# Moving one tile's PE transpose ahead of a pair of score steps in the start of an attention and MLP kernel

## The chip, the cores and the metric

The kernel runs on one core of a Trainium2 chip. The metric is device time in microseconds. All timed runs with more than one execution were fast, at a granted TensorE clock of 1.00.

## The reference, cut to what matters

```python
xn = _layernorm(x)                                   # x: 2048 x 512
q  = (xn @ wq) -> 32 heads of 2048 x 128
p  = softmax(q @ k_cache.T * 128 ** -0.5)            # 2048 keys per head
s  = concat_heads(p @ v_cache) @ wo
g  = silu(relu(xn @ w1 + b1) ** 2 @ w2 + b2)
return x + s * g
```

## The kernel before

Each engine has a program in a fixed order, and waits on semaphore counts where it needs another engine's result. The long steady state takes 512 query rows at a time through each head: scores on TensorE into `psA`, an exponential on ScalarE from `psA` into `pT`, then `pT` against `v` ("PV") on TensorE into `psO`. `psA` has two halves, so scores `pi` have to wait for exponential `pi - 2`.

Only the first head is different. Its 512 query rows come in four tiles of 128, counted from 0 here, and work starts on a tile as soon as it is there. A tile is normalised and scaled on VectorE (`xn_t`), transposed on TensorE, copied to `xnT` by VectorE, and projected for the first and the second head. Tile `qt` then makes two steps, scores `2*qt` and `2*qt + 1`, one per half of the keys.

```python
def first_transpose(i):                              # four 128x128 PE transposes
    for c in range(NDC):
        t_xT[i] = E(PE, partial(_peT, out=bankF(1)..., in_=xn_t[:, i, ...], ident=ident[:]),
                    deps=[t_xn[i], t_ident, tok_xT[0][i - 1] if i else None], ...)

# gen_scores(pi), first head only
qt, b = divmod(pi, 2)
for c in range(NKT // 2):                            # eight matmuls of 128 columns
    t = E(PE, partial(_mm_shared, out=psA[...], lhsT=kT[...], rhs=qt_sb[:, 0, qt*P:(qt+1)*P], ...),
          deps=[t_k0[b], t_q0[qt], t_exp[pi - 2] if pi >= 2 else None], ...)
...
t_exp[pi] = E(AC, partial(_act, out=pT[:, pi % NPT, :], in_=psA[...], func=ACT.Exp, ...),
              deps=[t, t_PV[pi - NPT] if pi >= NPT else None])

# the emission order of the start (cut)
second_proj(1)
gen_pv(0)
ln_bn(0, 3, 0, HD)
gen_scores(2)
ln_scale(0, 2)
first_transpose(2)
ln_bn(0, 3, HD, D)
gen_scores(3)
first_copy(2)
ln_rstd(0, 3, n=2)
first_proj(2)
first_evac(2)
second_proj(2)
gen_pv(1)
ln_scale(0, 3)
gen_scores(4)
first_transpose(3)
first_copy(3)
gen_scores(5)
```

The softmax here doesn't subtract the row's maximum and nothing guards it: scores larger than these inputs give would overflow.

Of the kernel before, what the change touches and what calls it, by code (L numbers as in the profile page):

```python
# [214 lines left out]
def bass_recurrent_scan__mha_block_cached__dense_activation_squared_relu__prompt_kernel(  # L215
# [87 lines left out]
    def bankF(i):  # L303
        return psF[:, i * 512:(i + 1) * 512]
# [45 lines left out]
    def ln_bn(j, i, c0=0, c1=D):  # L350
        jt = j * TPB + i
        k = 6 if c0 else 0
        t_bn[jt] = E(DV, partial(_bn_stats, out=st_t[:, i, k:k + 6], in_=x_ln[:, i, c0:c1]),
                     deps=[t_xl[jt], t_xn.get(jt - TPB), t_xr.get(jt - TPB)])
# [15 lines left out]
    def ln_scale(j, i):  # L370
        jt = j * TPB + i
        t_xn[jt] = E(DV, partial(_ts, out=xn_t[:, i, :], in0=x_ln[:, i, :],
                                 scalar1=mv_t[:, i, 0:1], scalar2=rstd[:, i:i + 1],
                                 op0=ALU.subtract, op1=ALU.mult),
                     deps=[t_xr[jt], t_xnr.get(jt - TPB)])
# [49 lines left out]
    def first_transpose(i):  # L425
        for c in range(NDC):
            t_xT[i] = E(PE, partial(_peT, out=bankF(1)[:, 0:256].bitcast(BF16)[:, c * P:(c + 1) * P],
                                    in_=xn_t[:, i, c * P:(c + 1) * P], ident=ident[:]),
                        deps=[t_xn[i], t_ident, tok_xT[0][i - 1] if i else None],
                        inc=(c == NDC - 1))  # L430
        t_xnr[i] = t_xT[i]
# [93 lines left out]
    def gen_scores(pi):  # L525
        g, k = divmod(pi, NPR)
        s2, i = pi % 2, g % NSL
        assert t_kfill[g] is not None and t_evac[g] is not None
        t = None
        if g == 0:  # L530
            qt, b = divmod(pi, 2)
            for c in range(NKT // 2):
                t = E(PE, partial(_mm_shared, out=psA[:, s2 * 1024 + c * P:s2 * 1024 + (c + 1) * P],
                                  lhsT=kT[:, 0, (b * NKT // 2 + c) * P:(b * NKT // 2 + c + 1) * P],
                                  rhs=qt_sb[:, 0, qt * P:(qt + 1) * P], start=True, stop=True),
                      deps=[t_k0[b], t_q0[qt], t_exp[pi - 2] if pi >= 2 else None],
                      inc=(c == NKT // 2 - 1))
        else:
            for n in range(2):
                tt = 2 * k + n  # L540
                t = E(PE, partial(_mm, out=psA[:, s2 * 1024 + n * 512:s2 * 1024 + (n + 1) * 512],
                                  lhsT=kT[:, i, tt * P:(tt + 1) * P], rhs=qt_sb[:, g % NQS, :],
                                  start=True, stop=True),
                      deps=[t_exp[pi - 2] if pi >= 2 else None, t_kfill[g], t_evac[g],
                            t_bankF[0] if pi == 0 else None],
                      inc=(n == 1))
        if k == NPR - 1:
            t_S_last[g] = t
        t_exp[pi] = E(AC, partial(_act, out=pT[:, pi % NPT, :],
                                  in_=psA[:, s2 * 1024:(s2 + 1) * 1024],  # L550
                                  func=ACT.Exp, scale=SM_SCALE),
                      deps=[t, t_PV[pi - NPT] if pi >= NPT else None])
# [373 lines left out]
    second_proj(1)  # L926
    gen_pv(0)
    ln_bn(0, 3, 0, HD)
    gen_scores(2)
    ln_scale(0, 2)  # L930
    first_transpose(2)
    ln_bn(0, 3, HD, D)
    gen_scores(3)
    first_copy(2)
# [104 lines left out]
```

## Time and profile before

| | before |
|---|---|
| median of 3 runs | 1238.17 us (1237.9 to 1238.31) |
| span of the profiled run | 1236.1 us |
| TensorE busy | 99% |
| ScalarE busy | 85% |
| PV 0 starts | 9.30 us |
| scores 5 start | 12.83 us |

The times below are read as starts of groups of matmuls. The profile models the end of a matmul, so a short wait between two groups on TensorE can lie under the modelled tail of the first one. It is then seen only where the distance between two starts exceeds the usual slot: 0.45 us for eight matmuls of 128 columns, 0.23 us for four. Below, such a usual distance is called a slot. In profile lines PE is TensorE's matmuls, PEld its weight loads, DVE VectorE, ACT ScalarE and POOL GpSimd; brackets at the end give the idle time just before and what ended it.

### The profile page before, as it was taken

To read this page: it belongs to the slowest core of one execution; us is meant where nothing else is said; L and a number is where in the kernel's file an instruction comes from. 1 tells how busy PE (TensorE), PEld (TensorE's weight loads), DVE (VectorE), ACT (ScalarE), POOL (GpSimd) and SP (SyncE) were. 2 spreads that over 40 slices of the span, in tenths; PEclk is the share of its full clock that TensorE was granted. 3 is DMA by queue.
4 is the path that set the end of the run, shared out by engine and by line. 5 is a ranking of instruction groups with operands and counts; after the bars stand their busy time and mean duration, and the time that the engine had idled before them with its cause. 6 is when DMAs were issued, how large, how long until landed. Compare 5 with 4: busy or idle time off the path is not lost.

```text
span 1236.1 us, 26728 instructions
## 1 busy us (share of the span) xinstructions
PE 1220.8 (99%) x11678; PEld 819.1 (66%) x11885; DVE 472.8 (38%) x953; ACT 1054.6 (85%) x1044; POOL 32.0 (3%) x73
## 2 busy tenths in 40 slices
PE   9999999999999999999999999999999999999998
PEld 7666666666666666666666666666666666666665
DVE  4453323244435332334444532333344333324333
ACT  7888888888888888888888888888888888888885
POOL 1010000000002000000000200000000000000000
PEclk9999999999999999999999999999999999999999
DMA  9999998787879897768779878787778788878771
GB/s 211 203 245 194 187 178 134 130 144 143 140 152 171 144 158 129 141 138 144 133 135 169 171 138 144 141 148 133 134 146 148 146 154 158 137 134 146 145 124 31
DMA packets 686868, 185.41 MB, mean 150 GB/s; under 512 B 673536, under 2 KB 685568, under 8 KB 686752
## 3 DMA queue, kind: packets, MB, share of 16 engines
q1 hardware_dynamic: 684656, 179.62, 80.0%
q0 software_dynamic: 1424, 3.81, 1.2%
q8 instruction: 94, 1.54, 0.6%
q10 hardware_dynamic: 672, 0.26, 0.1%
q14 instruction: 22, 0.18, 0.0%
HBM read 96.60 MB, written 2.10 MB: 80 GB/s over the span
## 4 chain that ended last, share of the span: by engine, by line
PE 98%; issue 1%; DVE 0%; DMA 0%; POOL 0%; DVEq 0%
PE psO L157 38%; PE psA L152 35%; PE psF L152 25%; PE psA L157 0%; DMA x_ln<-in_A_x_dram 0%; DVE out_t L165 0%; PE psF L196 0%; DVE tmp_t L175 0%; PE psO L152 0%; DVE xnT L179 0%; DVE st_t L200 0%; POOL rstd L165 0%; DVE xn_t L171 0%; DVE mv_t L204 0%; DVE ve_t L171 0%
## 5 line engine op out<-in xcount | busy, mean ns | idle before, releaser
L161 ACT ACTIVATE pT<-psA 128x1024 bf16<-128x1024 f32 x1024 | 1044.5, 1024 | 162.9 <-PE psA L152 117.6
L157 PEld LDWEIGHTS psO<-v_sb,pT 128*128 128x128 bf16 x8192 | 547.9, 98 | 240.3 <-issue 12.4
L157 PE MATMUL psO<-v_sb,pT 128*128 128x129 bf16 x8192 | 631.2, 220 | 0.5
L152 PE MATMUL psA<-qt_sb,kT 128*128 128x512 bf16 x1840 | 562.9, 379 | 10.1
L179 DVE COPY o_un<-psO 128x258 f32<-128x258 f32 x256 | 97.4, 422 | 399.5 <-PE psO L157 398.8
L152 PE MATMUL psF<-xnT,wq_sb 128*128 128x512 bf16 (+1 forms) x508 | 165.7, 374 | 0.4 <-DVE xnT L179 0.2
L152 PE MATMUL psF<-wo_all,oT 128*128 128x512 bf16 x478 | 163.2, 379 | 0.1
L152 PEld LDWEIGHTS psA<-qt_sb,kT 128*128 128x128 bf16 x2032 | 157.0, 98 | 0.0
L179 DVE CAST qt_sb<-psF 128x512 bf16<-128x512 f32 (+1 forms) x130 | 88.0, 677 | 97.3 <-PE psF L152 93.7
L165 DVE TENSOR_TENSOR o_bf<-o_un,rden 128x512 bf16<-128x512 f32 x128 | 88.6, 692 | 4.7 <-DVE rden L183 0.3
L152 PEld LDWEIGHTS psF<-xnT,wq_sb 128*128 128x128 bf16 x520 | 50.3, 98 | 60.0 <-issue 0.3
L171 DVE TENSOR_SCALAR r_t<-psF,b1f 128x512 bf16<-128x512 f32 x56 | 42.0, 750 | 117.4 <-PE psF L152 117.4
L152 PEld LDWEIGHTS psF<-wo_all,oT 128*128 128x128 bf16 x480 | 46.9, 98 | 56.4
L152 PE MATMUL psF<-xnT,w_sb 128*128 128x512 bf16 x224 | 77.1, 379 | 0.0
L152 PE MATMUL psF<-w_sb,h2T 128*128 128x512 bf16 x223 | 73.7, 379 | 0.0
L152 PEld LDWEIGHTS psF<-xnT,w_sb 128*128 128x128 bf16 x224 | 21.9, 98 | 26.4
L152 PEld LDWEIGHTS psF<-w_sb,h2T 128*128 128x128 bf16 x224 | 21.9, 98 | 26.4
L165 DVE TENSOR_TENSOR z_t<-psF,b2bc 128x512 f32<-128x512 f32 x16 | 11.1, 692 | 67.2 <-PE psF L152 62.0
L165 DVE TENSOR_TENSOR acc<-psF,acc 128x512 f32<-128x512 f32 x28 | 19.3, 689 | 30.0 <-PE psF L152 30.0
L208 POOL DMA_DIRECT2D out_dram<-out_t x12 | 6.7, 554 | 891.1 <-DVE out_t L165 891.1
L165 DVE TENSOR_TENSOR h2T<-r_t 128x512 bf16<-128x512 bf16 x56 | 23.8, 426 | 1.9
L183 DVE RECIPROCAL rden<-o_un 128x4 f32<-128x4 f32 x128 | 22.9, 179 | 4.4
(47 smaller groups left out, 165.2 us busy)
## 6 DMA issues: line engine op xcount, KB each, us to landing
v_sb<-in_A_v_cache_dram SPq DMA_DIRECT2D x127, 512.0 KB, 4.7
wq_sb<-in_A_wq_dram SPq DMA_DIRECT2D x127, 128.0 KB, 3.1
wo_all<-in_A_wo_dram SPq DMA_DIRECT2D x4, 1024.0 KB, 6.4
w_sb<-in_B_w_dram SPq DMA_DIRECT2D x14, 256.0 KB, 4.1
oT<-o_bf SPq DMA_TRANSPOSE x128, 4.0
x_t<-in_A_x_dram POOLq DMA_DIRECT2D x16, 128.0 KB, 3.5
kT<-in_A_k_cache_dram SPq DMA_TRANSPOSE x127, 4.5
x_ln<-in_A_x_dram SPq DMA_DIRECT2D x15, 128.0 KB, 4.0
```

Of the source, the lines that this page charges most:

```text
L152: return e.matmul(out, lhsT, rhs, start=start, stop=stop)
L157: return e.matmul(out, lhsT, rhs, start=start, stop=stop, skip_group_check=True)
L161: return e.activation(out, in_, func, bias=bias, scale=scale)
L165: return e.tensor_tensor(out, in0, in1, op)
L171: return e.tensor_scalar(out, in0, scalar1=scalar1, scalar2=scalar2, op0=op0, op1=op1)
L179: return e.tensor_copy(out, in_)
L183: return e.reciprocal(out, in_)
L208: return e.dma_start(out, in_)
```

## The change

The transpose of tile 2 (the third tile) goes ahead of scores 2, the first scores of its predecessor, tile 1. The intent: its copy on VectorE then runs while TensorE does scores 2 and 3, and the projection behind them need not wait for it.

```diff
     gen_pv(0)
     ln_bn(0, 3, 0, HD)
-    gen_scores(2)
     ln_scale(0, 2)
     first_transpose(2)
+    gen_scores(2)
     ln_bn(0, 3, HD, D)
     gen_scores(3)
```

## The prediction

> **What bounds the kernel now.** I read the page first: busy shares, then the chain that ended last.
>
> ```profile
> PE 1220.8 (99%) x11678; PEld 819.1 (66%) x11885; DVE 472.8 (38%) x953; ACT 1054.6 (85%) x1044; POOL 32.0 (3%) x73
> ...
> PE 98%; issue 1%; DVE 0%; DMA 0%; POOL 0%; DVEq 0%
> PE psO L157 38%; PE psA L152 35%; PE psF L152 25%; PE psA L157 0%; DMA x_ln<-in_A_x_dram 0%; DVE out_t L165 0%; PE psF L196 0%; DVE tmp_t L175 0%; PE psO L152 0%; DVE xnT L179 0%; DVE st_t L200 0%; POOL rstd L165 0%; DVE xn_t L171 0%; DVE mv_t L204 0%; DVE ve_t L171 0%
> ```
>
> TensorE's matmuls are 98% of the chain; ScalarE is busy 85%. The view of who waited for whom says whether anything but TensorE's own order holds it back:
>
> ```profile
> ACT pT L161 <- PE psA L152: 117.6, 397, 0.5
> ...
> PEld psO L157 <- issue: 12.4, 62, 0.2
> ```
>
> ScalarE waits for TensorE 397 times, while the steady state's weight loads wait only for "issue" (62 pauses of at most 0.2 us, no producer named). No DMA stands among TensorE's releasers. So a delay or gain in the start that survives until about 16 us should reach the end at its own size, neither grown nor absorbed.
>
> The change lies in that start: the first head pair, whose four query tiles are normalised, transposed and scored one by one. Timeline of before for PE, weight loads left out; columns are start, us, engine, line, op, tiles:
>
> ```profile
> 9.30 0.63 PE L157 MATMUL psO<-v_sb,pT 128*128 128x129 bf16 x8
> 9.77 0.61 PE L157 MATMUL psA<-qt_sb,kT 128*128 128x128 bf16 x8
> 10.21 0.39 PE L196 MATMUL psF<-ident,xn_t 128*128 128x128 bf16 x4
> 10.44 0.61 PE L157 MATMUL psA<-qt_sb,kT 128*128 128x128 bf16 x8
> 11.12 0.40 PE L152 MATMUL psF<-xnT,wq_sb 128*128 128x128 bf16 x4
> 11.35 0.39 PE L152 MATMUL psO<-xnT,wq_sb 128*128 128x128 bf16 x4
> 11.58 0.62 PE L157 MATMUL psO<-v_sb,pT 128*128 128x129 bf16 x8
> 12.03 0.61 PE L157 MATMUL psA<-qt_sb,kT 128*128 128x128 bf16 x8
> 12.60 0.40 PE L196 MATMUL psF<-ident,xn_t 128*128 128x128 bf16 x4
> 12.83 0.61 PE L157 MATMUL psA<-qt_sb,kT 128*128 128x128 bf16 x8
> ```
>
> In order: PV 0; scores 2; transpose of tile 2; scores 3; tile 2's two projections; PV 1; scores 4; transpose of tile 3; scores 5. From starts of groups in a row without a wait: eight matmuls take a slot of 0.45 us, four take 0.23. Two slots are longer. Scores 3 to projection is 0.68, so 0.23 of waiting; scores 4 to the next transpose is 0.57, so 0.12 of waiting. These waits end with other engines' work, in VectorE's and ScalarE's timelines:
>
> ```profile
> 9.44 0.40 DVE L171 TENSOR_SCALAR xn_t<-x_ln,mv_t,rstd 128x512 bf16<-128x512 bf16 x1
> 9.75 0.42 DVE L200 BATCH_NORM_STATS2 st_t<-x_ln 128x6 f32<-128x256 bf16 x1
> 10.64 0.42 DVE L179 COPY xnT<-psF 128x512 bf16<-128x512 bf16 x1 [0.47 <-PE psF L196]
> ...
> 12.13 0.41 DVE L171 TENSOR_SCALAR xn_t<-x_ln,mv_t,rstd 128x512 bf16<-128x512 bf16 x1 [0.28 <-POOL rstd L165]
> ```
>
> ```profile
> 10.41 1.94 ACT L161 ACTIVATE pT<-psA 128x1024 bf16<-128x1024 f32 x2 [0.25 <-PE psA L157]
> 12.68 1.94 ACT L161 ACTIVATE pT<-psA 128x1024 bf16<-128x1024 f32 x2 [0.33 <-PE psA L157]
> ```
>
> The copy of tile 2's transpose ends at 11.06 and the projection starts 0.06 later: that is the 0.23. The scaling of tile 3 ends at 12.54, its transpose starts at 12.60: that is the 0.12. ScalarE runs exponentials 2 and 3 from 10.41 to 12.35, each 1.02 long and so 0.92 apart, with idle gaps of 0.25 and 0.33 in front of this pair and the next.
>
> **What the Trainium skill says.** "TensorE: Matmul & The Clock Gate", section "What overlaps and what doesn't", has matmuls in strict order. The trace agrees: the groups run in program order, and TensorE waits at 11.12 although PV 1, behind the projection, needs only an exponential that ended near 10.16. So a transpose put first makes the scores wait with it. The same page, "Part 4: PE-mode transpose", gives about 275 ns for a 128x128 transpose in a kernel and notes that a DVE copy must follow. Here one takes 219 ns, they are pipelined, and four hold a slot of 0.23; I use that. "Perfetto Trace Analysis", "Tensor Engine Instruction (MATMUL, LD_WEIGHTS)", says that a matmul's reported end is estimated and that semaphore propagation is hidden. Therefore I use start-to-start times and measured hand-over gaps: VectorE to TensorE 0.05 to 0.06, TensorE's last end to its reader 0.03 to 0.04, and ScalarE to TensorE about 0.06 (PV 0 starts at 9.30, and the exponential before it ran from 8.22 to 9.24).
>
> **The change part by part.** No instruction is added or removed. The four transposes of tile 2 (a 0.23 slot) exchange places with the eight matmuls of scores 2 (0.45). VectorE's, ScalarE's and POOL's orders stay the same.
>
> 1. A new wait. TensorE's slot after PV 0 opens at 9.77, but tile 2's scaled rows end at 9.84; plus 0.05, the transposes start at 9.89. Wait: 0.12.
> 2. Scores 2 start at 9.89 + 0.23 = 10.12 instead of 9.77, 0.35 later, and end at 10.73. Scores 3 start at 10.57 instead of 10.44.
> 3. The transposes end at 9.89 + 0.40 = 10.29; the copy runs from 10.33 to 10.75 instead of 10.64 to 11.06, 0.31 earlier. VectorE is free then, its statistics ending at 10.17.
> 4. The projection is ready at 10.81, but TensorE comes to it only at 10.57 + 0.45 = 11.02. The old wait of 0.23 vanishes; against the new 0.12, TensorE is 0.10 to 0.11 ahead (11.02 for 11.12).
> 5. Projections and PV 1 follow without a wait; scores 4 start at 11.93 for 12.03. They need exponential 2 finished: it now starts at 10.73 + 0.03 = 10.76 and ends at 11.78, ready at 11.84. It fits with 0.09 to spare.
> 6. Tile 3's chain (aggregate, POOL's two small operations, scaling) hangs on the copy of step 3 and moves by the same 0.31, so its rows end near 12.23 and can be used at 12.28. TensorE reaches its transpose at 12.38: the old 0.12 is gone too, and 0.22 is gained at this point.
> 7. Then scores 5, in TensorE's order due at 12.61. They write the psA half that exponential 3 reads. The exponentials were delayed by 0.35, so it ends at 12.70 instead of 12.35 and releases it at 12.76. A new wait of 0.15 takes most of it back: scores 5 start at 12.76 for 12.83. Net gain **0.07 us**.
> 8. Afterwards exponential 4 starts at 12.60 (0.92 after exponential 3; scores 4 are done at 12.54) for 12.68. Everything up to scores 6 follows TensorE's order with 0.07 less; ScalarE has 0.88 of idle before 15.49, so its delay is used up.
>
> Sum: +0.12 (new wait for the scaling), -0.23 (copy), -0.12 (tile 3's scaling), +0.15 (psA half), about -0.08; from the rounded starts -0.07. On the path that is 1238.17 - 0.07 = **1238.1 us**.
>
> **The rivals.**
> - The wait for the scaling is the only thing that survives. If the delayed exponentials hold TensorE longer (a hand-over of 0.15 instead of 0.06, or the second exponential slower while VectorE copies from PSUM), scores 5 start later than 12.83 and the change costs up to about 0.12. For it: margins in steps 5 and 7 are under 0.1 us. Against it: the hand-over was seen as 0.06. It would make 1238.2 to 1238.3.
> - The full gain of 0.22 survives because scores 5 don't wait. That needs exponential 3 free by 12.61, so ending at 12.55 at most, but two exponentials starting after scores 2 take 1.94, from 10.76. It would make 1237.95; I give it little.
> - ScalarE is the engine that sets the start, so its 0.35 delay comes through whole: 1238.5. Against it stand the 0.25, 0.33 and 0.88 us of ScalarE idle while it waits for TensorE; the second and third absorb it.
> - A shift of a tenth of a microsecond changes how later DMAs meet, or the 62 issue pauses. The waits of before show no DMA on TensorE's path, and the pauses belong to a stream whose length is unchanged. One or two pauses more or fewer would be 0.2 to 0.4 us either way, as much as the repeated runs differ by.
>
> **Range and chances.** The three runs spread over 0.41 us (1237.9 to 1238.31), so a median of a few runs moves by perhaps 0.2. All the mechanisms lie between -0.22 and +0.35. Allowing another 0.3 for a differing build, I take 1237.5 to 1238.8. A 2% change is 24.8 us; the entire stretch from the moved transpose to scores 6 (10.21 to 14.85) is under 5 us, so even losing it twice over would not be 2%. Within 2%: 0.99, the rest split evenly.
>
> **What would show it right or wrong.** In the changed profile: the transposes of tile 2 first at about 9.89, VectorE's scaling as releaser; scores 2 near 10.12; exponential 2 near 10.76 with idle near 0.6 instead of 0.25; the copy at 10.33 and no wait of the projection on xnT, which starts at 11.02; tile 3's transpose near 12.38; scores 5 near 12.76, held by pT's exponential; the steady state's waits unchanged. Wrong in sign if scores 5 start after 12.83. Wrong altogether if the time differs by over 0.7 us: that would need a difference in the steady state, for which I see no cause.

## The result

| | before | changed |
|---|---|---|
| median, same rounds, 6 runs each | 1238.02 us | 1238.09 us |
| lowest to highest | 1237.9 to 1238.31 | 1237.8 to 1238.53 |
| ratio, 95% interval | | 1.0 (0.9988 to 1.0013) |

A ratio is the mean time of one kernel's fast runs over that of the other's fast runs of the same rounds, so it is not quite the ratio of the medians. 1238.09 lies on the predicted 1238.1. That match is luck and confirms nothing: 1238.1 was 0.07 below a median of before that was itself 1238.17 then and 1238.02 here, and in these rounds the changed kernel's median is 0.07 above it. The effect is small against runs of one kernel, which differ by several tenths. The trace has to say whether the reasons hold.

First the page of the changed kernel, its busy shares and its chain that ended last:

```profile
PE 1231.9 (100%) x11885; PEld 819.5 (66%) x11885; DVE 472.3 (38%) x953; ACT 1053.4 (85%) x1044; POOL 32.0 (3%) x73
...
PE 99%; DVE 0%; issue 0%; POOL 0%; DVEq 0%; POOLq 0%
```

TensorE seems to have worked 11.1 us more. It has not. The page of before lists 11678 matmuls beside 11885 weight loads, this one 11885 of both: 207 matmul records were missing from the first trace. The change has no part in it: three later traces of the changed kernel list 11678 again (1220.7 to 1221.0 us busy); in all, exactly 207 are missing in nine of the 13 traces. A difference in busy time is to be read with the counts beside it.

The view of who waited for whom in the changed kernel:

```profile
ACT pT L161 <- PE psA L152: 118.0, 397, 0.5
...
PEld psO L157 <- issue: 12.5, 62, 0.2
```

The steady state is as before: 118.0 for 117.6 us, and again 62 pauses. Now the start, TensorE's timeline without weight loads in the changed kernel:

```profile
9.48 0.63 PE L157 MATMUL psO<-v_sb,pT 128*128 128x129 bf16 x8
10.07 0.40 PE L196 MATMUL psF<-ident,xn_t 128*128 128x128 bf16 x4
10.30 1.06 PE L157 MATMUL psA<-qt_sb,kT 128*128 128x128 bf16 x16
11.20 0.39 PE L152 MATMUL psF<-xnT,wq_sb 128*128 128x128 bf16 x4
11.42 0.39 PE L152 MATMUL psO<-xnT,wq_sb 128*128 128x128 bf16 x4
11.64 0.62 PE L157 MATMUL psO<-v_sb,pT 128*128 128x129 bf16 x8
12.10 0.61 PE L157 MATMUL psA<-qt_sb,kT 128*128 128x128 bf16 x8
12.54 0.39 PE L196 MATMUL psF<-ident,xn_t 128*128 128x128 bf16 x4
12.95 0.62 PE L157 MATMUL psA<-qt_sb,kT 128*128 128x128 bf16 x8
```

VectorE's scaling and copy of tile 2 and scaling of tile 3, then ScalarE's exponentials 2 to 5, then the weight loads of scores 5, same run:

```profile
9.62 0.40 DVE L171 TENSOR_SCALAR xn_t<-x_ln,mv_t,rstd 128x512 bf16<-128x512 bf16 x1
...
10.51 0.42 DVE L179 COPY xnT<-psF 128x512 bf16<-128x512 bf16 x1 [0.16 <-PE psF L196]
...
11.99 0.41 DVE L171 TENSOR_SCALAR xn_t<-x_ln,mv_t,rstd 128x512 bf16<-128x512 bf16 x1
```

```profile
10.95 3.77 ACT L161 ACTIVATE pT<-psA 128x1024 bf16<-128x1024 f32 x4 [0.61 <-PE psA L157]
```

```profile
12.94 0.45 PEld L157 LDWEIGHTS psA<-qt_sb,kT 128*128 128x128 bf16 x8 [0.18 <-ACT pT L161]
```

The whole stretch is 0.18 us later than before, because PV 0 itself, which stands ahead of the moved instructions, started at 9.48 and not at 9.30. Counted from PV 0 the picture is clean. "Predicted" is the time of the prediction less its 9.30:

| us after PV 0 starts | before | predicted | changed |
|---|---|---|---|
| transpose of tile 2 | 0.91 | 0.59 | 0.59 |
| scores 2 | 0.47 | 0.82 | 0.82 |
| copy of tile 2 | 1.34 | 1.03 | 1.03 |
| exponential 2 | 1.11 | 1.46 | 1.47 |
| projection of tile 2 | 1.82 | 1.72 | 1.72 |
| scores 4 | 2.73 | 2.63 | 2.62 |
| transpose of tile 3 | 3.30 | 3.08 | 3.06 |
| scores 5 | 3.53 | 3.46 | 3.47 |
| PV 4 | 6.44 | | 6.39 |
| last 58 matmuls of the kernel | 1217.94 | | 1217.89 |

The last row comes from these lines, of before and of the changed kernel:

```profile
1227.24 5.86 PE L152 MATMUL psA<-wo_all,oT 128*128 128x512 bf16 x58
```

```profile
1227.37 5.86 PE L152 MATMUL psA<-wo_all,oT 128*128 128x512 bf16 x58
```

Scores 5 start 0.06 us earlier, PV 4 (the one behind scores 6 and 7) and the last matmuls 0.05. In absolute time the last matmuls are 0.13 later (1227.37 for 1227.24), which is the 0.18 of PV 0 less the 0.05.

### The profile page after: what moved, and what is told of

Same layout as the page of the kernel before. It is cut to its first block, busy times and chain, and to the rows that moved or that the text cites. A ratio compares the mean times of both kernels' runs of the same rounds, so it can differ in the third digit from the quotient of the medians.

```text
span 1236.2 us, 26935 instructions
## 1 busy us (share of the span) xinstructions
PE 1231.9 (100%) x11885; PEld 819.5 (66%) x11885; DVE 472.3 (38%) x953; ACT 1053.4 (85%) x1044; POOL 32.0 (3%) x73
## 4 chain that ended last, share of the span: by engine, by line
PE 99%; DVE 0%; issue 0%; POOL 0%; DVEq 0%; POOLq 0%
PE psO L157 38%; PE psA L152 36%; PE psF L152 25%; PE psA L157 0%; DVE out_t L165 0%; PE psO L196 0%; DVE tmp_t L175 0%; PE psF L196 0%; PE psO L152 0%; DVE qt_sb L179 0%; POOL warm L187 0%; POOL mhalf L187 0%; DVEq L119 0%; POOLq L1024 0%
## 5 line engine op out<-in xcount | busy, mean ns | idle before, releaser
L161 ACT ACTIVATE pT<-psA 128x1024 bf16<-128x1024 f32 x1024 | 1043.4, 1023 | 163.7 <-PE psA L152 118.0
L152 PE MATMUL psA<-qt_sb,kT 128*128 128x512 bf16 x2032 | 604.4, 379 | 0.0
L152 PE MATMUL psF<-xnT,wq_sb 128*128 128x512 bf16 (+1 forms) x520 | 168.7, 374 | 0.1
L165 DVE TENSOR_TENSOR z_t<-psF,b2bc 128x512 f32<-128x512 f32 x16 | 11.1, 691 | 67.2 <-PE psF L152 67.2
```

The source lines that it names most:

```text
L152: return e.matmul(out, lhsT, rhs, start=start, stop=stop)
L161: return e.activation(out, in_, func, bias=bias, scale=scale)
L165: return e.tensor_tensor(out, in0, in1, op)
```

## The experiments

My theory: the change swaps waits in TensorE's queue with a sum of about -0.06 us, and this reaches the end undiminished, under a variation of the start that has nothing to do with it. The main rival: the order affects PV 0's start too, and the change costs what the medians show.

**The two kernels again.** Both unaltered, more than once; first one of each.

> The changed kernel, unaltered, to get a second profile and a narrower interval. My theory: the change gives TensorE 0.06 us, measured from the start of PV 0 (L157 psO x8, the first one): scores 5 start 3.47 us after it (before: 3.53), the steady state some 0.05 us earlier than before. What the first profile showed on top, PV 0 itself 0.18 us later, is a variation of the first key load and not of the change: here PV 0 may start anywhere from 9.25 to 9.55. Time against before: ratio 1.0 within 0.0005. Rival, that the change really costs 0.07 us as the medians read: PV 0 again 0.18 later, and a ratio above 1.

> The kernel before, unaltered, for a second profile. Theory: scores 5 start 3.53 us after PV 0 again, the projection of tile 2 at 1.82 and the transpose of tile 3 at 3.30 after it, whatever PV 0's own start (9.25 to 9.55). Rival, that the order decides PV 0's start: PV 0 at 9.30 again.

After again: 1237.97 us median of 5 runs, before in the same rounds 1237.97 of 9, ratio 0.9999 (0.9986 to 1.0013). Scores 5 stood at 3.47 after PV 0 (13.02 and 9.55) in the changed kernel and at 3.53 (12.81 and 9.28) in the one before; before again had the projection at 1.82, but the transpose of tile 3 at 3.29 where 3.30 was expected. But PV 0 started at 9.55 and 9.28. With the kernels below, all three with the old order now had PV 0 at 9.28 to 9.30 and all six with the new at 9.42 to 9.62. That spoke for the rival.

> The kernel before, unaltered. In the profiles so far PV 0 started at 9.28 to 9.30 in all three kernels with the old order, at 9.42 to 9.62 in all six with the new. Theory: chance, since everything there runs before the moved instructions: it goes with the moment at which TensorE's matmuls get short (314 to 219 ns) and with the landing of the first keys. Then PV 0 can start past 9.4 here too. Rival, that the order sets it: 9.28 to 9.30 again in this and in before_4.

> The changed kernel, unaltered. Theory: PV 0's start varies with the clock's moment and the key load alone, so it can be near 9.3 here; and whatever it is, scores 5 start 3.47 after it. Rival, that the order sets it: 9.42 or later again in this and in after_4, and the times of these rounds 0.1 to 0.2 us above the kernel before.

> As before_3: a further profile and five times of the kernel before.

> As after_3: a further profile and five times of the changed kernel.

The pattern did not hold. In these four it is the other way round: PV 0 at 9.68 and 9.61 in the kernel before, at 9.25 and 9.26 in the changed one.

| | PV 0 starts | scores 5 after it | last matmuls after it | median of 5 |
|---|---|---|---|---|
| before_3 | 9.68 | 3.52 | 1217.94 | 1238.14 us |
| before_4 | 9.61 | 3.53 | 1217.94 | 1237.99 us |
| after_3 | 9.25 | 3.46 | 1217.89 | 1238.01 us |
| after_4 | 9.26 | 3.46 | 1217.89 | 1237.91 us |

All four are "same" (ratios 0.9999 to 1.0). The rival falls: either order has PV 0 early and late. What makes the start vary shows in TensorE's timeline of the first key transposes. This is before_4, where the transposes were short early (219 ns in the median) and the second half of the keys landed late:

```profile
6.57 0.62 PE L196 MATMUL psO<-ident,kT 128*128 128x128 bf16 x8 [0.47 <-DMA kT<-in_A_k_cache_dram]
```

And this is early_rows, described next, without a wait for a DMA there but with slow matmuls: the same eight transposes took 0.90 instead of 0.62, and the median transpose of the keys 314 ns where a fast one takes 219.

```profile
6.08 0.90 PE L196 MATMUL psO<-ident,kT 128*128 128x128 bf16 x8
```

So both the landing of a load and the moment at which the matmuls become short move PV 0, over 9.25 to 9.68 us in all runs: 0.43 us, seven times the effect of the change. Two pairs of traces separate them. The transposes of tile 0 start at 5.67 both in after_4 and in early_rows (whose own edits act later), here in this order, without a wait for a DMA:

```profile
5.67 0.40 PE L196 MATMUL psF<-ident,xn_t 128*128 128x128 bf16 x4
```

```profile
5.67 0.62 PE L196 MATMUL psF<-ident,xn_t 128*128 128x128 bf16 x4
```

The first projection then starts at 6.68 and 6.89, PV 0 at 9.26 and 9.47: slow matmuls alone, 0.21 us. In before_again and before_4 the same transposes start at 5.69 and 5.70 and take 0.40; then the key transposes start at 5.93 and, with their load late, at 6.57, PV 0 at 9.28 and 9.61: a late load alone, 0.33 us.

**Rows of tile 2 earlier.** The new wait before the transpose is for the scaled rows. They can be had sooner: the small variance operation on VectorE, and the scaling before tile 3's statistics. To the changed kernel:

```diff
-    ln_rstd(0, 2)
+    ln_rstd(0, 2, eng=DV)
...
-    ln_bn(0, 3, 0, HD)
     ln_scale(0, 2)
+    ln_bn(0, 3, 0, HD)
```

> The change, and tile 2's scaled rows made earlier: its small variance operation on VectorE instead of POOL, and its scaling ahead of the first half of tile 3's statistics. Theory: the new wait of 0.12 before the transpose of tile 2 falls to about 0.02, so everything up to exponential 3 is 0.10 earlier, and scores 5 start 3.36 after PV 0 (changed kernel 3.47, before 3.53), still held by exponential 3. Rival, that exponential 3 isn't what holds scores 5: they follow the transpose of tile 3 directly, whose rows aren't earlier, and stay near 3.47. The time is 0.1 lower than the changed kernel's at most, which the rounds can't resolve: ratio 1.0 to before within 0.0005.

TensorE in this run, the transpose of tile 2 and scores 5:

```profile
9.96 0.40 PE L196 MATMUL psF<-ident,xn_t 128*128 128x128 bf16 x4
...
12.84 0.62 PE L157 MATMUL psA<-qt_sb,kT 128*128 128x128 bf16 x8
```

With PV 0 at 9.47, the transpose is at 0.49 (wait 0.02) and scores 5 at 3.37, against 3.47. PV 4 is at 6.29 and the last matmuls at 1217.79, 0.10 earlier than in the changed kernel and 0.15 earlier than before. The rival, that scores 5 depend on tile 3's rows and stay, is out. The time: 1237.79 us median of 5, against 1237.97 of before and of the changed kernel in the same rounds; ratio to before 0.9998 (0.9986 to 1.0011). The result is correct. In the trace it is the best correct version run here; by the interval of its times it is the same.

**Exponential 3 made short, with both orders.** If the wait of scores 5 for exponential 3 takes back most of the gain, shortening that one exponential must help the changed kernel and do nothing for the one before. The result is wrong in 512 columns of one step. The same edit was made to both kernels:

```diff
+    t_pT3 = E(GP, partial(_memset, out=pT[:, 3, 512:1024], val=1.0))
...
-        t_exp[pi] = E(AC, partial(_act, out=pT[:, pi % NPT, :],
-                                  in_=psA[:, s2 * 1024:(s2 + 1) * 1024],
+        w_exp = 512 if pi == 3 else 1024
+        t_exp[pi] = E(AC, partial(_act, out=pT[:, pi % NPT, 0:w_exp],
+                                  in_=psA[:, s2 * 1024:s2 * 1024 + w_exp],
                                   func=ACT.Exp, scale=SM_SCALE),
-                      deps=[t, t_PV[pi - NPT] if pi >= NPT else None])
+                      deps=[t, t_PV[pi - NPT] if pi >= NPT else t_pT3 if pi == 3 else None])
```

> The change, with exponential 3 taken over 512 of its 1024 columns (wrong result on purpose; the rest of its tile is filled with ones by POOL early), so that it ends about 0.45 us sooner and frees its half of psA before scores 5 come to it. Theory: the wait of scores 5 for exponential 3 is what takes back 0.15 to 0.18 us; without it they follow tile 3's transpose directly and start 3.29 us after PV 0 instead of 3.47. Rival, something else holds scores 5 (tile 3's rows, TensorE's order): 3.47 unchanged.

> The kernel before with the same short exponential 3 (wrong result on purpose). Theory: there exponential 3 was done long before scores 5 came, so nothing moves: scores 5 start 3.53 us after PV 0. With the run of the changed kernel the gain of the change is then 0.24 us in place of 0.06. Rival, a shorter exponential helps both alike: scores 5 here near 3.35.

Transpose of tile 3 and scores 5, first in the changed order, PV 0 at 9.62:

```profile
12.68 0.39 PE L196 MATMUL psF<-ident,xn_t 128*128 128x128 bf16 x4
12.90 0.61 PE L157 MATMUL psA<-qt_sb,kT 128*128 128x128 bf16 x8
```

and in the old order, PV 0 at 9.28:

```profile
12.57 0.40 PE L196 MATMUL psF<-ident,xn_t 128*128 128x128 bf16 x4
12.80 0.61 PE L157 MATMUL psA<-qt_sb,kT 128*128 128x128 bf16 x8
```

Changed: scores 5 one slot after the transpose, at 3.28 instead of 3.47. Before: 3.52, nothing moved. With this wait away the change is worth 3.52 - 3.28 = 0.24 us, and it keeps that: PV 4 at 6.19 against 6.43, the last matmuls at 1217.70 against 1217.94. This is the term that turns a gain of 0.24 into one of 0.06. The two single times, 1237.97 (changed order) and 1237.88 us, don't show it; their starts differ by 0.34 us.

**The same move one step further.** The next transpose, of tile 3, also put ahead of its predecessor's scores. To the changed kernel:

```diff
     ln_scale(0, 3)
-    gen_scores(4)
     first_transpose(3)
+    gen_scores(4)
```

> The change, and the same move one step further on: tile 3's transpose ahead of scores 4. Theory: its rows are usable 2.97 us after PV 0, while TensorE comes to it at 2.62, so the new wait is 0.35 us; scores 4 start at 3.20 instead of 2.62, scores 5 at 3.65 instead of 3.47, no longer held by exponential 3 (free at 3.46). A loss of 0.18 against the changed kernel: the same move costs where the rows are not ready, and the copy's wait that it could save isn't there. Rival, that putting a transpose first always helps because the copy runs sooner: scores 5 at 3.47 or less.

The transpose of tile 3, then scores 4 and 5 merged, with PV 0 at 9.42:

```profile
12.40 0.40 PE L196 MATMUL psF<-ident,xn_t 128*128 128x128 bf16 x4 [0.20 <-DVE xn_t L171]
12.63 1.06 PE L157 MATMUL psA<-qt_sb,kT 128*128 128x128 bf16 x16
```

The transpose waits until 2.98 (expected 2.97), and scores 4 start at 3.21. Scores 5 are the second half of a merged group, so one slot of 0.45 later at 3.66 (worked out; expected 3.65). PV 4 is at 6.57, 0.18 later than in the changed kernel, and the last matmuls at 1218.07, 0.18 later too. The same exchange costs here, because the rows are ready 0.36 us after TensorE comes for them (2.98 against the changed kernel's 2.62).

**A delay of known size.** Does what happens in the start reach the end at its own size? To the changed kernel:

```diff
-    t_bankF[:] = [t_q0[3], t_b1[0]]
     gen_pv(3)
+    t_x = None
+    for x in range(36):
+        t_x = E(PE, partial(_mm, out=bankF(0)[:, 0:P], lhsT=warm[:], rhs=warm[:], start=True,
+                            stop=True), deps=[t_q0[3], t_warm], inc=(x == 35))
+    t_bankF[:] = [t_x, t_b1[0]]
```

> The change, and 36 needless matmuls of 128 columns on TensorE after PV 3, into a bank that is free then (the result stays right). At 56 ns each they take 2.0 us. Theory: what happens to TensorE in the start reaches the end at its own size, so the time is 1240.1 us, 2.0 more than the changed kernel. Rival, that the long steady state has room to absorb a later start (then the 0.06 us would have been absorbed there too): under 0.5 us more.

The added matmuls, and scores 6 behind them:

```profile
15.08 2.17 PE L152 MATMUL psF<-warm 128*128 128x128 bf16 x36
17.09 1.06 PE L157 MATMUL psA<-qt_sb,kT 128*128 128x128 bf16 x16
```

```profile
1229.48 5.86 PE L152 MATMUL psA<-wo_all,oT 128*128 128x512 bf16 x58
```

17.09 - 15.08 is 2.01 us. The last matmuls start 1219.90 us after PV 0 (1229.48 and 9.58), 2.01 later than in the changed kernel, and the time is 1239.98 us (median of 4), 2.01 above the 1237.97 of the changed kernel in the same rounds (against before: ratio 1.0016, 1.0002 to 1.003). The steady state absorbed nothing of it.

**All times together.** The two unaltered kernels ran 21 times (changed) and 34 times (before), with means of 1238.01 and 1238.05 us. The difference of -0.04 has the sign and size of the trace's -0.05, but since single runs spread over 0.7 us and the calls were on different chips, it is no proof of it. The traces show it: the last matmuls stand 1217.94 us after PV 0 in four profiles of before, 1217.89 in four of the changed kernel, without exception. They also show where the spread of the times comes from. Each trace belongs to one execution with a time of its own. That time less the start of PV 0 is 1228.60 or 1228.61 us in the four traces of before (before_again, a single look, among them) and 1228.52 to 1228.59 in the four of the changed kernel. The eight times lie between 1237.77 and 1238.28 us; with PV 0's start taken off, 0.09 us of spread is left, and the means differ by 0.05, the size of the change's effect.

## Why the prediction was right

- **Bound and passage** (TensorE sets the time, a shift of the start arrives at its own size): right; the delay of 2.01 us arrived as 2.01, and 0.05 us arrived as 0.05.
- **Steps 1 to 3** (a new wait of 0.12, scores 2 later by 0.35, the copy earlier by 0.31): right to 0.01 us, counted from PV 0. The wait has no line of its own in the view of waits, against the forecast that VectorE's scaling would show as releaser: the modelled end of PV 0 (9.48 + 0.63 = 10.11) covers it, and the pause of the weight loads there, 0.14 us, is shorter than any wait that these views of the start list (0.15 and up). It is 0.12 all the same, 0.59 less the old start of 0.47, and it ends 0.05 after the scaling (9.62 + 0.40 = 10.02); in early_rows, with the scaling earlier, it fell to 0.02.
- **Step 4** (the projection stops waiting): right, 0.90 us from scores 2 to the projection is exactly two slots.
- **Steps 5 and 6**: right, with scores 4 at 2.62 and the transpose of tile 3 at 3.06, one slot on.
- **Step 7** (scores 5 wait for exponential 3): the mechanism was right and is shown by the pair of short exponentials. The term was slightly undersized: 12.95 - 12.54 less the slot of 0.23 is 0.18 us, predicted 0.15. Tile 3's transpose came 0.02 earlier than thought, and exponential 3 0.01 later.
- **Step 8**: right. Exponential 4 follows exponential 3 without a pause, at 3.31 by the 0.92 between starts (predicted 3.30), scores 6 start at 5.49 instead of 5.55, and ScalarE idles 0.90 us before exponential 6.
- **Sum**: 0.12 - 0.23 - 0.12 + 0.18 = -0.05 us, predicted -0.07.
- **The rivals**: only the waits surviving, the full 0.22 surviving, and ScalarE setting the start are all excluded by scores 5 at 3.47 and by PV 4 at 6.39. The fourth, that later DMAs or the pauses shift, is excluded too: from PV 4 to the last matmuls it is 1211.50 us in both kernels, with 62 pauses in both.
- **The number**: 1238.09 on 1238.1 was luck, as said above. The range's upper end did not follow from its own terms: 1238.17 + 0.35 + 0.2 + 0.3 is 1239.02, not 1238.8; all timed runs of the two unaltered kernels lay between 1237.77 and 1238.53, inside both.
- **What the prediction did not foresee**: its absolute times in the start (9.89 and so on) missed by 0.18, since PV 0's own start varies. It had put the spread of runs down as a number of 0.41 us without asking where in the trace it arises; it arises mostly before PV 0.

## What to carry to other kernels

In an in-order queue, an instruction moved forward brings its own wait with it; list every wait removed and every wait added along the queue, up to where the delayed consumer (here an exponential that frees a PSUM half) comes round again, and only then add up. For an effect smaller than the spread of the times, align the traces on an event just before the change and compare distances, in more than one profile of each kernel. Nine profiles here looked like a systematic shift of the start by the order, and four more showed that it was none. Where a trace and a time belong to the same execution, take the varying start off the time too.

## What the Trainium skill lacked or had wrong

- "TensorE: Matmul & The Clock Gate", "Back-to-back issue gap", gives about 81 ns per matmul for a stream of weight-load and matmul pairs at N=128, and about 131 ns at N=512. Here eight such pairs take a slot of 0.45 us, 56 ns each, and 36 take 2.01 us, 56 ns each; at N=512 the 16 that start at 1222.19 in the changed kernel take 3.46 us, 216 ns each. The measurement decides: these are the page's figures for an isolated gap.
- The same page, "Part 4: PE-mode transpose", has about 275 ns in a kernel; here a transpose takes 219 ns when fast, 314 when slow, and four in a row hold TensorE for 0.23 us.
- The same page, Part 1 on the HAM clock gate, lets the moment of the clock's change vary from run to run and puts the whole ramp penalty under 1% of a typical kernel's span. How much a kernel's time varies by it from run to run, it doesn't say. Here that moment, seen as transposes of 314 or 219 ns, and the landing of the first keys together move the start of PV 0 over 0.43 us between profiles of nearly identical kernels, 0.03% of the span, of which slow matmuls alone made 0.21 in one pair.
- "Perfetto Trace Analysis", "Tensor Engine Instruction (MATMUL, LD_WEIGHTS)", says that a matmul's end is estimated. It doesn't draw the consequence met here: under that modelled end, a wait of 0.12 us between two groups got no line among the waits, and shows only in start-to-start distances. It doesn't warn that matmul records can be missing from a trace (207 in nine of 13 traces here), which made TensorE look 11.1 us busier after the change.
